# Walking the inverse's tile with heads innermost, and storing the solved inverse with blocks outermost

## The chip, the cores and the metric

One core of one Trainium2 chip runs the whole program. The metric is device microseconds (us) of one execution, from the first instruction to the last with what lies around them; a kernel's time is the median of several executions.

## The reference, cut to what matters

The first half is a recurrence over 768 steps for 4 batches x 8 heads, with a 40 x 40 state for each head; the second half is a small network on its output.

```python
for t in range(S):                       # S = 768
    y[:, :, t] = einsum('bhd,bhde->bhe', rt, state)
    Sa = einsum('bhde,bhe->bhd', state, at)
    state = state * wt[:, :, None, :] - einsum('bhd,bhe->bhde', Sa, bt)
    state = state + einsum('bhd,bhe->bhde', vt, kt)
x = y.transpose(0, 2, 1, 3).reshape(4, 768, 320)
u = x + (relu(x.T @ w_tok1) @ w_tok2).T
out = u + relu(u @ w_ch1) @ w_ch2
```

## The kernel before, in words

**The recurrence in chunks.** Time is cut into chunks of 64 steps; a group is one chunk of one batch with its 8 heads, 48 groups in all, and a pair is two neighbouring groups. Inside a chunk the steps depend on each other through a triangular 64 x 64 matrix for each head, and the kernel needs its inverse. The matrix is split into blocks of 32. The diagonal blocks of eight groups together (one set, six sets in all) are inverted by VectorE (DVE) in one go; the block off the diagonal is then put in by TensorE (PE).

**Function `t_a` (one call for each pair).** TensorE forms the products `px` (L679) in PSUM. For each half h the function `side` then issues on ScalarE (ACT): `e3`, three copies with the sign turned, from `px` into the tile `Dg` (L709), one over 128 partitions and two over 32 each; `e2` and `e4`, which copy other blocks (L691 on DVE for the first pairs, L693 on ACT later); and last, on DVE, `e1` (L699), after which the PSUM bank of `px` is given back. `Dg` is [128, 32 (s), 32 (n)]: s is the column in the block, n counts the 32 heads of the set. One `e3` writes four heads, two apart, of all 32 columns. Before the change it goes head by head: the writes step 128 bytes, the reads of `px` run in line.

**Function `t_solve` (one call for each set).** `first` (L760) is a DVE transpose of `Dg` into `DT`; a chain of small DVE steps (L782 to L818) solves into `Tl`; `o1` (L838) is a DVE transpose of `Tl` into `TBt`, the solved inverse, which reuses the tile `DT`; `o2` (L843) makes the second form `TBn`. Before the change `TBt` is [128, t, n] with the head n innermost, so the 32 values of one head's row lie 128 bytes apart. `o1` reads `Tl` in steps of 128 bytes and writes in line; `o2` does both in line.

**Users of `TBt`.** In the first two sets (16 groups) `merge` multiplies with it (`tbt`, L924) and adds a result into it (L935). For groups 0 to 23 `t_b` copies it into the block diagonal tile `TBD` in four copies of 32 x 128 (L963 on ACT, L964 on DVE) and uses it as the moving operand of the matmuls `pe` (L971). For the other 24 groups, in 12 pairs, `t_b2` does the same with copies of 32 x 256 (L1047, L1048) and matmuls `pe` (L1054). The matmuls `pt` (L999, L1084) that follow take `TBn` as the weights. `ph` (L1015, L1103) needs `TBD` whole.

**What sets the order.** A planner written in the kernel runs when the program is built: every operation carries an engine and a cost in ns written by hand, and the planner lays out one fixed order for each engine. It also puts matmuls without use (the fillers, L384) into the TensorE queue where it expects that engine to be idle. Engines run their queues in order. The costs written beside the operations are the same before and after the change.

**The rest.** `t_chain` and `t_y` carry the state from chunk to chunk; `t_mlp` is the network, whose matmuls L1567 and L1675 fill TensorE from about 340 us on, batch after batch, beside the remaining groups.

Of the kernel before, what the change touches and what calls it, by code (L numbers as in the profile page):

```python
# [13 lines left out]
AF = mybir.ActivationFunctionType  # L14
# [266 lines left out]
def tile_kernel(ctx, tc, r, k, v, w, a, b, wt1, wt2, wc1, wc2, wT, aT, kbT, vT, rT, vt, out, dbg=None):  # L281
    nc = tc.nc
# [3 lines left out]
    NP = H // 2  # L286
    NG = B * NC
    L = 32
# [29 lines left out]
    for h in range(2):  # L318
        sl = slice(h * 64, h * 64 + 64)
# [10 lines left out]
    def zbufs(shape, name, n):  # L330
        ts_ = [ctile(shape, f"{name}{i}") for i in range(n)]
        for t in ts_:
            nc.gpsimd.memset(t, 0.0)
        return ts_
# [9 lines left out]
    Tl3 = Tl[:, 0:1024].rearrange("p (j t) -> p j t", j=L)  # L344
    nc.gpsimd.memset(Tl.rearrange("p (a b) -> p a b", b=33)[:, :, 0], 1.0)
    NAB, NKP = K["nab"], K["nkp"]
    Dg = zbufs([128, L, L], "Dg", 1)[0]
# [14 lines left out]
    TBD = zbufs([128, 2 * NP, 128], "TBD", 1)[0]  # L362
# [218 lines left out]
    def noff(g):  # L581
        return NOF[g // 4][:, g % 4]
# [17 lines left out]
    def t_a(q):  # L600
        g0 = 2 * q
        si, ci = SETOF[g0]
        rank = rank_a(g0)
        early = g0 < K["eb"]
        d = {}
# [5 lines left out]
        def get_at():  # L611
            if "at" not in d:
                d["at"] = ap_.tile([128, 2 * NP, DP], F32, tag="AT", name=f"AT{q}", bufs=ATN)
                for z in range(2):
                    st[g0 + z]["at"] = d["at"][:, z * NP:(z + 1) * NP]
            return d["at"]
# [45 lines left out]
        now = yield None  # L662
# [10 lines left out]
        now = yield None  # L673
        P.rel(R_px, now)

        def pxm(z, p, h):
            def f():
                rows, cols = slice(h * 64, h * 64 + D), slice(p % 2 * 64, p % 2 * 64 + 64)
                nc.tensor.matmul(px[h][cols, 2 * z + p // 2, :], lhsT=Ac[q][rows, z, p, :], rhs=KBp[q][rows, p, z, :], start=True, stop=True)  # L679
            return ("PE", (57, 128, "E"), f)  # L680
        now = yield [pxm(z, p, h) for z in range(2) for p in range(NP) for h in (p % 2, 1 - p % 2)]
# [13 lines left out]
        def side(h):  # L695
            px_ = px[h]

            def e1():
                tt(out=get_at()[:, h::2, 0:64], in0=px_[:, :, 0:64], in1=low.unsqueeze(1).to_broadcast([128, NP, 64]), op=ALU.mult)  # L699

            def e2():
                if "n21" not in d:
                    d["n21"] = pair_n21[q] = ap_.tile([128, 2 * NP, L], F32, tag="N21", name=f"N21_{q}", bufs=ATN)
                    for z in range(2):
                        st[g0 + z]["n21"] = d["n21"][:, z * NP:(z + 1) * NP]
                neg(d["n21"][:, h::2], px_[:, :, 64:96])

            def e3(sl, c0):
                return ("ACT", 190 if sl.start == 0 else 392, lambda: nc.scalar.activation(  # L709
                    out=Dg[sl, :, ci * NP + h:(ci + 2) * NP:2].rearrange("p s n -> p n s"),  # L710
                    in_=px_[sl, :, c0:c0 + L], func=AF.Copy, scale=-1.0))

            def e4():
                o_ = NOF[g0 // 4][:, g0 % 4:g0 % 4 + 2].rearrange("p c n t -> p (c n) t")
                neg(o_[:, h::2], px_[:, :, 96:128])
            e3s = [e3(slice(0, 128), 64), e3(slice(L, 2 * L), 96), e3(slice(3 * L, 4 * L), 96)]
            if ea:
                yield [("DVE", 205, e2)] + [("DVE", 205, e4)] * (si < PEM)
                now = yield e3s
            else:  # L720
                now = yield e3s[:1] + [("ACT", 320, e2)] + e3s[1:] + [("ACT", 174, e4)] * (si < PEM)
            P.set(done[h], now)
            now = yield [("DVE", 400, e1)]
            P.rel(tks[h], now)
            yield at_ev
            now = yield None
            P.join(("at", q), 2, now, *[lambda now, z=z: P.set(AT_done[g0 + z], now) for z in range(2)])
        now = yield None
# [4 lines left out]
        now = yield None  # L733
# [10 lines left out]
    def t_solve():  # L744
        now = yield -5.0
        P.set(Dg_free[0], now)
        for i, n in enumerate(SETS):
# [7 lines left out]
            d = {}  # L755
# [5 lines left out]
            now = yield [("DVE", 1810, first)]  # L761
            P.set(Dg_free[i + 1], now)
            DT = d["DT"]
            DT3 = DT[:, 0:1024].rearrange("p (t s) -> p t s", t=L)
# [69 lines left out]
                        yield [op]  # L834

            def o1():
                TBt = DT3
                nc.vector.transpose(out=TBt, in_=Tl3.rearrange("p j t -> p t j"))  # L838
                TB[i] = [TBt]

            def o2():
# [3 lines left out]
            now = yield [("DVE", 1945, o1), ("DVE", 1158, o2)]  # L845
# [66 lines left out]
    def merge(g, ci, n21, TBt, TBn, rank):  # L912

        d = {}
        cs = slice(ci * NP, (ci + 1) * NP)
        yield rank - K["mrg"]
        yield R_et1
        d["pm"], tk = yield from bank("w", [128, 3, NP, L], f"pm{g}")

        def mm(z, lhs, rhs):  # L920
            def f1(p, q):
                def f():
                    sl = slice(q * L, (q + 1) * L)
                    nc.tensor.matmul(d["pm"][sl, z, p, :], lhsT=lhs(sl, p, q), rhs=rhs(sl, p, q), start=True, stop=True)  # L924
                return ("PE", (36, 32, "D"), f)
            return [f1(p, q) for p in range(NP) for q in range(4)]
        tbt = lambda sl, p, q: TBt[sl, :, ci * NP + p]
        tbn = lambda sl, p, q: TBn[sl, :, ci * NP + p]
        et = lambda sl, p, q: ET1[sl, p, :]
        yield mm(0, lambda sl, p, q: noff(g)[sl, p, :] if q % 2 else n21[sl, p, :], tbt)  # L930
        yield [("ACT", 260, lambda: nc.scalar.activation(out=ET1[:, :, 16:32], in_=d["pm"][:, 0, :, 16:32], func=AF.Copy, scale=half[:, 0:1]))]
        yield mm(1, tbn, et) + mm(2, et, tbn)

        def add(dst, z, c0):
            return ("DVE", 180, lambda: tt(out=dst, in0=d["pm"][:, z, :, c0:c0 + 16], in1=dst, op=ALU.add))  # L935
        now = yield [add(TBt[:, 16:32, cs].rearrange("p t n -> p n t"), 1, 16),
                     add(TBn[:, 0:16, cs].rearrange("p j n -> p n j"), 2, 0)]
        P.rel(tk, now)
        P.rel(R_et1, now)
        P.set(merged[g], now)  # L940
        yield rank

    def t_b(g):
        bi, c = divmod(g, NC)
        o = st[g]
        i, ci = SETOF[g]
# [5 lines left out]
        TBt, TBn = TB[i]  # L952
        d = {"tbd": TBD[:, g % 2 * NP:(g % 2 + 1) * NP]}
# [5 lines left out]

        def tbd(q):  # L960
            sl = slice(q * L, (q + 1) * L)
            dst, src = d["tbd"][sl, :, sl], TBt[sl, :, ci * NP:(ci + 1) * NP].rearrange("p t n -> p n t")
            ops = {"A": ("ACT", 425, lambda: nc.scalar.copy(out=dst, in_=src)),  # L963
                   "D": ("DVE", Port(285), lambda: nc.vector.tensor_copy(out=dst, in_=src)),  # L964
                   "P": ("POOL", 460, lambda: nc.gpsimd.tensor_copy(out=dst, in_=src))}
            return [ops[z] for z in K["tbd"][g >= K["tbd_early"]][q]]

        def pe(p, h):
            def f():
                q0, q1 = h * 64, h * 64 + 32  # L970
                nc.tensor.matmul(d["pe"][q0:q0 + L, p, :], lhsT=n21[q1:q1 + L, p, :],  # L971
                                 rhs=TBt[q1:q1 + L, :, ci * NP + p], start=True, stop=True)
            return ("PE", (50, 80, "D"), f)

        def etc(h):
# [12 lines left out]
        now = yield None  # L988
# [4 lines left out]
        now = yield [etc(0), etc(1)]  # L993
# [13 lines left out]
        now = yield [pt(p, h) for p in range(NP) for h in range(2)]  # L1007
        P.rel(R_et, now)
        yield tbd_done
        now = yield [tin(0), tin(1)]  # L1010
# [15 lines left out]
        now = yield [("ACT", 490, huc)]  # L1026
# [5 lines left out]
    def t_b2(q):  # L1032
        g0 = 2 * q
        i, ci = SETOF[g0]
# [5 lines left out]
        TBt, TBn = TB[i]  # L1040
        cs = slice(ci * NP, (ci + 2) * NP)
        d = {}

        def tbd(r):
            sl = slice(r * L, (r + 1) * L)
            dst, src = TBD[sl, :, sl], TBt[sl, :, cs].rearrange("p t n -> p n t")
            ops = {"A": ("ACT", 700, lambda: nc.scalar.copy(out=dst, in_=src)),  # L1047
                   "D": ("DVE", Port(490), lambda: nc.vector.tensor_copy(out=dst, in_=src))}  # L1048
            return [ops[z] for z in K["tbd"][g0 >= K["tbd_early"]][r]]

        def pe(n, h):
            def f():
                q0, q1 = h * 64, h * 64 + 32
                nc.tensor.matmul(d["pe"][q0:q0 + L, n, :], lhsT=n21[q1:q1 + L, n, :],  # L1054
                                 rhs=TBt[q1:q1 + L, :, ci * NP + n], start=True, stop=True)
            return ("PE", (50, 80, "D"), f)

        def etc(z, h):
# [14 lines left out]
        now = yield None  # L1073
# [4 lines left out]
        now = yield [etc(z, h) for z in range(2) for h in range(2)]  # L1078
# [13 lines left out]
        now = yield [pt(n, h) for n in range(2 * NP) for h in range(2)]  # L1092
        P.rel(R_et, now)
        yield tbd_done
        now = yield [tin(0), tin(1)]
        P.rel(tk, now)
        for z in range(2):
# [17 lines left out]
            now = yield [("ACT", 490, huc)]  # L1115
# [617 lines left out]
    with tc.manual_schedule():  # L1733
# [5 lines left out]
        for g in range(NG):  # L1739
            si, ci = SETOF[g]  # L1740
# [167 lines left out]
```

## Time and profile before

| what | value |
|---|---|
| median of 3 executions | 824.08 us (818.68 to 826.0) |
| profiled execution | 826.04 us, of which the span is 824.2 us |
| busy: PE, DVE, ACT | 776.5, 610.9, 486.0 us |
| mean granted TensorE clock | 0.973 |

Busy time of an engine is the time in which one of its instructions runs. Matmul ends are modelled, so a busy PE isn't PE at its peak. "Granted clock" is 1.00 at TensorE's upper level and 0.50 at its lower one. A filler counts as busy. In the lists a tile stands by its name: `DT` is the tile that `TBt` lies in, `m` and `px` are PSUM tiles.

### The profile page before, as it was taken

The page shows a single profiled execution, that of the slowest core. Times are in us where ns is not written, and L with a number is a line of the kernel's source. Part 1 is how long each engine was busy: PE and PEld are TensorE (multiplying, and loading weights), DVE is VectorE, ACT ScalarE, POOL GpSimd, SP SyncE. Part 2 cuts the span into 40 slices and gives each one's busy share as a digit, 9 for nine tenths or more (in the row PEclk, how much of TensorE's full clock was granted, in tenths as well). Part 3 has the DMA queues.
Part 4 walks back from the last instruction along what each step waited for, and adds up shares of the span by engine and source line. Part 5 has one row for each costly group of instructions (what it writes and reads, how often), then busy time and mean ns, then how long its engine had stood idle before and what let it go on. Part 6 is the DMA issues. An engine that isn't in the chain of part 4 may idle for free. (4 is left out here: it accounts for less than half of the span.)

```text
span 824.2 us, 27584 instructions
## 1 busy us (share of the span) xinstructions
PE 776.5 (94%) x11353; PEld 709.3 (86%) x11353; DVE 610.9 (74%) x1493; ACT 486.0 (59%) x1479; POOL 67.1 (8%) x143
## 2 busy tenths in 40 slices
PE   6797999888989989989999999999999999999997
PEld 6696888777878878879899899999999999998996
DVE  7999598998999878977879898499754433535342
ACT  5747887888778865765855746643654343443111
POOL 4000000000001110100101010001000010000000
PEclk9997897999999999989999999999999999999999
DMA  8964656778477975463677557244565534244341
GB/s 239 276 204 137 216 182 191 209 233 251 142 249 208 266 231 155 124 184 115 193 226 230 174 176 222 66 131 135 192 174 166 168 100 123 95 141 163 109 151 52
DMA packets 69077, 144.23 MB, mean 175 GB/s; under 512 B 8016, under 2 KB 45904, under 8 KB 65872
## 3 DMA queue, kind: packets, MB, share of 16 engines
q1 hardware_dynamic: 62608, 95.20, 39.1%
q0 software_dynamic: 6336, 47.19, 17.9%
q8 instruction: 92, 1.51, 0.8%
q14 instruction: 41, 0.34, 0.2%
HBM read 115.81 MB, written 26.54 MB: 173 GB/s over the span
## 5 line engine op out<-in xcount | busy, mean ns | idle before, releaser
L1675 PE MATMUL m<-ut,wg_c 128*128 128x384 f32 x768 | 162.5, 348 | 2.1 <-issue 2.0
L1567 PE MATMUL m<-wg_c,hd 128*128 128x320 f32 x864 | 157.3, 322 | 0.1
L1567 PEld LDWEIGHTS m<-wg_c,hd 128*128 128x128 f32 x864 | 131.3, 191 | 4.9 <-DVE hd L1687 2.2
L1675 PEld LDWEIGHTS m<-ut,wg_c 128*128 128x128 f32 x768 | 131.2, 189 | 2.2 <-DVE x L1715 0.5
L1685 ACT ACTIVATE hd<-m 128x384 fp32r<-128x384 f32 x96 | 47.2, 492 | 124.7 <-PE m L1675 118.1
L1687 DVE SCALAR_TENSOR_TENSOR hd<-m,hd 128x384 fp32r<-128x384 f32 x96 | 53.4, 556 | 57.9 <-ACT hd L1685 57.2
L1715 DVE TENSOR_TENSOR x<-m,x 128x320 f32<-128x320 f32 x96 | 46.8, 488 | 53.2 <-PE m L1567 52.5
L709 ACT ACTIVATE Dg<-px 128x128 f32<-128x128 f32 x144 | 56.5, 393 | 14.9 <-PE px L679 10.5
L1165 PE MATMUL pq<-RBs,VSs 104*104 104x128 f32 x384 | 57.8, 289 | 0.8 <-ACT VSs L1280 0.7
L1165 PEld LDWEIGHTS pq<-RBs,VSs 104*104 104x104 f32 x384 | 49.9, 180 | 3.2 <-ACT VSs L1280 1.5
L384 PE MATMUL yb<-ident 128*128 128x192 bf16 x479 | 46.3, 253 | 3.2 <-POOL ident masks.py:199 1.8
L1305 PE MATMUL yb<-KB,RM 128*64 128x40 f32 x768 | 47.3, 230 | 0.7 <-DVE RM L1222 0.7
L1307 PE MATMUL yb<-VSs,RBs 104*64 104x40 f32 x768 | 46.6, 229 | 0.0
L384 PEld LDWEIGHTS <-ident 128*128 128x128 bf16 x479 | 41.2, 101 | 4.9 <-issue 2.2
L1305 PEld LDWEIGHTS yb<-KB,RM 128*64 128x64 f32 x768 | 39.7, 137 | 4.9 <-issue 2.6
L1172 ACT COPY Gb<-pq 104x256 f32<-104x256 f32 x96 | 34.4, 373 | 15.1 <-PE pq L1165 13.6
L1307 PEld LDWEIGHTS yb<-VSs,RBs 104*64 104x64 f32 x768 | 39.7, 137 | 0.0
L397 DVE TENSOR_TENSOR cv_c<-cv_c 128x384 f32<-128x384 f32 (+3 forms) x72 | 36.5, 522 | 1.9 <-ACT cv_c L1408 1.5
L307 PE MATMUL pU<-ident,Gb 104*104 104x104 f32 x176 | 30.2, 268 | 8.0 <-DVE Gb L1259 3.5
L1200 POOL TENSOR_TENSOR RM<-Gb,upp 64x128 f32<-64x128 f32 x45 | 23.6, 531 | 169.2 <-ACT Gb L1172 169.0
L1250 PE MATMUL pS<-W2s,KB 128*40 128x40 f32 x704 | 33.6, 207 | 1.5 <-ACT W2s L1230 0.7
L307 PEld LDWEIGHTS pU<-ident,Gb 104*104 104x104 f32 x176 | 17.7, 132 | 19.1 <-ACT Gb L1263 6.5
(170 smaller groups left out, 1719.2 us busy)
## 6 DMA issues: line engine op xcount, KB each, us to landing
wg_c<-sG POOLq DMA_DIRECT2D x16, 1152.0 KB, 6.2
wg_c<-sG POOLq DMA_DIRECT2D x16, 960.0 KB, 5.4
KBp<-in_kbT_dram SPq DMA_DIRECT2D x24, 448.0 KB, 5.8
RBs<-in_rT_dram SPq DMA_DIRECT2D x48, 224.0 KB, 4.4
wg_t<-sT POOLq DMA_DIRECT2D x8, 1152.0 KB, 5.9
VSs<-in_vT_dram SPq DMA_DIRECT2D x48, 182.0 KB, 3.6
sKB<-KT SPq DMA_DIRECT2D x48, 160.0 KB, 3.1
KB<-sKB SPq DMA_DIRECT2D x48, 160.0 KB, 4.4
```

The lines of the kernel that those rows point to most:

```text
L307: nc.tensor.matmul(out_, lhsT=in_, rhs=idn, start=True, stop=True, is_transpose=True)
L384: nc.tensor.matmul(yb[:, 320:512], lhsT=zf[:, 0:128], rhs=zf[:, 0:192], start=True, stop=True)
L397: return [(e, Port(60 + f * n / 0.96 if e == "DVE" else 140 + 2.24 * n), lambda e=e: engines[e].tensor_tensor(out=out_(), in0=a_(), in1=b_ ...
L709: return ("ACT", 190 if sl.start == 0 else 392, lambda: nc.scalar.activation(out=Dg[sl, :, ci * NP + h:(ci + 2) * NP:2].rearrange("p s n - ...
L1165: nc.tensor.matmul(stepped(d["pq"][0:DP, p, 0:64], 144, 2), lhsT=vs[:, gi * 2 + p, :], rhs=rb[:, gi * 2 + p, :].rearrange("p (h t) -> p h ...
L1305: nc.tensor.matmul(dst, lhsT=rms[g - 1 + z][:, h, :], rhs=o["kb"][:, h, :], start=True, stop=False)
L1307: nc.tensor.matmul(dst, lhsT=o["rb"][:, h // 2, q0:q0 + 64], rhs=o["vs"][:, h // 2, 64:DP], start=False, stop=True)
L1567: nc.tensor.matmul(d[key], lhsT=lhs(i, a_), rhs=rhs(i, b_), start=i == 0 and j == 0, stop=i == n - 1 and j == 2)
L1675: nc.tensor.matmul(pt, lhsT=mm_[q][0], rhs=mm_[q][1], start=q == 0, stop=q == len(mm_) - 1)
L1685: nc.scalar.activation(out=hid[key][:, 0], in_=pt, func=AF.Relu)
L1687: now = yield [("DVE", dve(TB_), lambda: nc.vector.scalar_tensor_tensor(out=hid[key][:, 1], in0=pt, scalar=0.0, in1=hid[key][:, 0].bitcast ...
L1715: now = yield [("DVE", dve(320), lambda: tt(out=x()[:, i], in0=d[("c2", g, i)], in1=x()[:, i], op=ALU.add))]
```

## The change

Two layouts are turned, and nothing is added or taken away: the number and the order of the instructions stay.

- `e3`: the same elements go from `px` to `Dg`, in another order. Now the four heads are innermost: writes in runs of four, 8 bytes apart, then a step of 128 bytes; reads of `px` in PSUM step 512 bytes inside a run.
- `o1`: `TBt` is now [128, n, t], blocks outermost. The transpose still reads `Tl` in steps of 128 bytes and now also writes in steps of 128 bytes.
- Every user of `TBt` takes the new view, so that it reads (and in L935 also writes) in line: `tbt` of the matmuls L924, the first addition of L935, the copies L963, L964, L1047 and L1048, the moving operand of L971 and L1054.

```diff
             def e3(sl, c0):
                 return ("ACT", 190 if sl.start == 0 else 392, lambda: nc.scalar.activation(
-                    out=Dg[sl, :, ci * NP + h:(ci + 2) * NP:2].rearrange("p s n -> p n s"),
-                    in_=px_[sl, :, c0:c0 + L], func=AF.Copy, scale=-1.0))
+                    out=Dg[sl, :, ci * NP + h:(ci + 2) * NP:2],
+                    in_=px_[sl, :, c0:c0 + L].rearrange("p n s -> p s n"), func=AF.Copy, scale=-1.0))
...
             def o1():
-                TBt = DT3
-                nc.vector.transpose(out=TBt, in_=Tl3.rearrange("p j t -> p t j"))
+                TBt = DT[:, 0:1024].rearrange("p (n t) -> p n t", t=L)
+                nc.vector.transpose(out=TBt.rearrange("p n t -> p t n"), in_=Tl3.rearrange("p j t -> p t j"))
...
-        tbt = lambda sl, p, q: TBt[sl, :, ci * NP + p]
+        tbt = lambda sl, p, q: TBt[sl, ci * NP + p, :]
...
-        now = yield [add(TBt[:, 16:32, cs].rearrange("p t n -> p n t"), 1, 16),
+        now = yield [add(TBt[:, cs, 16:32], 1, 16),
...
-            dst, src = d["tbd"][sl, :, sl], TBt[sl, :, ci * NP:(ci + 1) * NP].rearrange("p t n -> p n t")
+            dst, src = d["tbd"][sl, :, sl], TBt[sl, ci * NP:(ci + 1) * NP]
...
-                                 rhs=TBt[q1:q1 + L, :, ci * NP + p], start=True, stop=True)
+                                 rhs=TBt[q1:q1 + L, ci * NP + p, :], start=True, stop=True)
...
-            dst, src = TBD[sl, :, sl], TBt[sl, :, cs].rearrange("p t n -> p n t")
+            dst, src = TBD[sl, :, sl], TBt[sl, cs]
...
-                                 rhs=TBt[q1:q1 + L, :, ci * NP + n], start=True, stop=True)
+                                 rhs=TBt[q1:q1 + L, ci * NP + n, :], start=True, stop=True)
```

## Rows read from the trace of the kernel before

**Rows 1.** Page: busy time with share and count; granted clock in 40 slices.

```profile
PE 776.5 (94%) x11353; PEld 709.3 (86%) x11353; DVE 610.9 (74%) x1493; ACT 486.0 (59%) x1479; POOL 67.1 (8%) x143
...
PEclk9997897999999999989999999999999999999999
```

**Rows 2.** Windows: length; busy PE, PEld, DVE, ACT, POOL; granted clock; DMA share; GB/s.

```profile
0.00:60.00 60.00, 47.74 (x626) 43.61 (x627) 55.18 (x130) 36.56 (x103) 10.64 (x32) 1.00 0.85 242
60.00:340.00 280.00, 256.94 (x5140) 226.07 (x5137) 245.06 (x614) 216.69 (x691) 16.27 (x31) 0.94 0.69 206
340.00:600.00 260.00, 255.02 (x3407) 235.69 (x3406) 212.64 (x503) 154.00 (x463) 24.65 (x50) 0.98 0.53 164
600.00:745.00 145.00, 143.60 (x1728) 132.40 (x1726) 65.88 (x181) 63.76 (x187) 11.84 (x23) 1.00 0.46 136
```

**Rows 3.** Groups by line and form: total us, mean ns; idle before. `e3`.

```profile
L709 ACT ACTIVATE Dg<-px 32x128 f32<-32x128 f32 x96 | 37.4, 390 | 1.5
...
L709 ACT ACTIVATE Dg<-px 128x128 f32<-128x128 f32 x48 | 19.1, 398 | 13.4 <-PE px L679 10.5 <-DVE noff L691 2.3
```

**Rows 4.** Timeline, 33 to 37 us: start, length, instruction, idle before it.

```profile
33.23 2.46 ACT L709 ACTIVATE Dg<-px 128x128 f32<-128x128 f32 x6
...
35.96 0.42 DVE L699 TENSOR_TENSOR AT<-px,low 128x256 f32<-128x256 f32 x1
...
36.14 0.90 PE L307 MATMUL pk<-ident,KBp 104*128 104x104 f32 x8 [1.37 <-ACT Dg L709]
36.29 1.97 DVE L760 STREAM_TRANSPOSE DT<-Dg 128x1024 f32<-128x1024 f32 x1
```

**Rows 5.** Groups by line and form: copies, additions, transposes of the inverse.

```profile
L963 ACT COPY TBD<-DT 32x128 f32<-32x128 f32 x53 | 21.8, 412 | 3.1 <-DVE DT L935 2.3
...
L1047 ACT COPY TBD<-DT 32x256 f32<-32x256 f32 x28 | 18.2, 649 | 0.4
...
L838 DVE STREAM_TRANSPOSE DT<-Tl 128x1024 f32<-128x1024 f32 x6 | 12.0, 1998 | 0.0
...
L964 DVE COPY TBD<-DT 32x128 f32<-32x128 f32 x43 | 11.7, 272 | 0.7
...
L1048 DVE COPY TBD<-DT 32x256 f32<-32x256 f32 x20 | 7.6, 378 | 0.4
L843 DVE STREAM_TRANSPOSE TBn<-Tl 128x1024 f32<-128x1024 f32 x6 | 7.4, 1226 | 0.0
...
L935 DVE TENSOR_TENSOR DT<-pm,DT 128x64 f32<-128x64 f32 x16 | 4.4, 274 | 3.4 <-PE pm L924 3.3
```

**Rows 6.** Groups by line and form: the nearest instructions without long steps.

```profile
L1005 ACT COPY TBD<-pt 32x128 f32<-32x128 f32 x48 | 12.2, 255 | 1.1 <-PE pt L999 0.5
...
L1260 DVE TENSOR_TENSOR Gb<-pS,PC 40x80 f32<-40x80 f32 x44 | 10.3, 234 | 0.7
...
L1402 ACT ACTIVATE cv_c<-cv_c 128x384 f32<-128x384 f32 x12 | 6.7, 558 | 0.5 <-DMA cv_c<-in_moe_w_ch_dram 0.4
...
L1402 ACT ACTIVATE cv_c<-cv_c 128x320 f32<-128x320 f32 x12 | 6.0, 500 | 0.1
...
L1403 DVE TENSOR_SCALAR cv_c<-cv_c 128x384 int32<-128x384 int32 x12 | 4.2, 353 | 0.1
...
L1403 DVE TENSOR_SCALAR cv_c<-cv_c 128x320 int32<-128x320 int32 x12 | 3.8, 318 | 0.0
...
L693 ACT ACTIVATE noff<-px 128x128 f32<-128x128 f32 x8 | 2.2, 278 | 0.1
```

**Rows 7.** Groups by line and form: the small matmuls of the later pairs.

```profile
L1084 PE MATMUL pt<-ET,TBn 32*32 32x32 f32 x384 | 13.1, 217 | 0.0
L1054 PE MATMUL pe<-DT,N 32*32 32x32 f32 x384 | 13.1, 228 | 0.0
```

**Rows 8.** Chain that ended last, in order of time: start, length, what.

```profile
711.53 1.00 PE pe L1054 x32
```

**Rows 9.** Windows, columns as in rows 2: one stretch with a low clock.

```profile
120.00:140.00 20.00, 18.82 (x362) 16.62 (x360) 16.41 (x47) 13.52 (x44) 0.00 (x0) 0.74 0.64 187
```

## The prediction, made before the changed kernel was run

> **What bounds the kernel now.** I read the page's busy time first, then a table of windows by stage, then the groups by line and form, and a piece of the timeline where an engine waits for a touched line. TensorE is busy 94% of the span [rows 1], so the question is when it is not. The windows answer it [rows 2]. In 340 to 600 and 600 to 745 us it is idle 260.00 - 255.02 = 5.0 and 145.00 - 143.60 = 1.4 us: there only work taken from TensorE itself shortens anything, and DVE and ACT have room. In the first 60 us it is idle 12.3 us, in 60 to 340 us 23.1 us, and here DVE is busy 92% and 88%, ACT 61% and 77%. So time given back on DVE and ACT before 340 us can reach the end, up to these 35 us of idle time, and after 340 us nearly none of it. The touched lines and their durations are in [rows 3], [rows 5] and [rows 7]; [rows 4] shows that one of them, L709, stands on a path in the prologue: six `e3` in a row take 2.46 us, the last `e1` (L699) comes behind them, and both TensorE's next transposes (idle 1.37 us) and the first set's transpose L760 start after it. The granted clock is a second bound: it falls to the lower level in a few stretches before 420 us [rows 1, 9], and in them a busy TensorE does its work at half speed.
>
> **The change part by part.** The number and order of the instructions stay, and no wait is added or removed, no queue is passed. What changes is how long each takes. I sum against the profiled execution, 826.04 us, and take the same sum off the median of 824.08, which is 0.24% less.
>
> *`e3`, 144 instructions.* Now 390 ns over 32 partitions and 398 over 128 [rows 3], with writes in steps of 128 bytes. The same engine evicting the same size from PSUM with writes in line takes 255 (L1005) and 278 ns (L693) [rows 6], so the write step costs some 120 to 135 ns. After the change the writes come in runs of four, 8 bytes apart. A run through SBUF in 8-byte steps is shown by L1402, as a read: 558 ns for 384 and 500 for 320 elements, 0.91 ns for each more, no dearer than it should be, so I expect the write penalty to go. But the reads of PSUM now step 512 bytes, which no row shows. Bounds: 255 (a read for free) and 390 + 135 = 525 ns (the read pays what the write paid, and the write keeps paying). I take 280 ns, near the rows from PSUM without long steps, since the step that these rows show as dear is one of SBUF; -0.11 us each.
> Prologue (36 of the 144): six in a row lose 0.66 us; the last six before L760 pass that on [rows 4], earlier pairs only in part, since DVE is 92% busy beside them. Value -1.0 us, bounds 0 and -2.6 (four pairs of 0.66). In 60 to 340 us 66 of them give ACT 7.3 us; the 42 later ones lie beside a busy TensorE and count nothing.
>
> *Copies into `TBD`.* On ACT 412 ns for 128 and 649 for 256 elements [rows 5]: 1.85 ns for each more element, against 0.91 in L1402. Carried down, L1402 gives 326 and 442 ns; L1005's 255 is the lower end. I take 326 and 442: -86 ns x 53 = -4.6 us, of which 50 copies (-4.3) lie before 340 us, and -207 ns x 28 = -5.8 us, all after 340 us. On DVE 272 and 378 ns; L1403, one source and one output in SBUF, costs 0.55 ns for each more element and gives 213 and 283: -59 x 43 = -2.5 us and -95 x 20 = -1.9 us (the latter after 340 us). No gain at all would be the other end.
>
> *`o1` and the addition L935.* `o1` reads in 128-byte steps and takes 1998 ns where `o2`, in line, takes 1226 [rows 5]: 0.75 ns for each element. With the write stepped too it could stay (+0) or add as much again (+0.77 us). L935 of before is the nearest row: it reads and writes `TBt` in 128-byte steps and takes 274 ns for 64 elements, against 234 for 80 in L1260, or about 217 for 64. That is 0.89 ns for each element for both steps together; they overlap. So `o1` goes to about 1226 + 0.89 x 1024 = 2.14 us, +0.14 us x 6, three of them before 340 us: +0.4. L935 loses its 57 ns: 16 x 0.057 = -0.9 us.
>
> *What of this reaches the end in 60 to 340 us.* ACT gets 7.3 + 4.3 = 11.6 us back of 216.7, DVE 2.5 + 0.9 - 0.4 = 3.0 of 245.1. Counted only where TensorE happens to be idle (8% of the stretch) that is 1.2 us; were every microsecond on the path, more than 11. Waits gather where these engines are late, so I take one and a half times the former: -1.8 us, bounds 0 and -8. The rest hides under TensorE's own work and its fillers, whose number is fixed; what is late next is TensorE itself.
>
> *Small matmuls.* The moving operand of `pe` now lies in line. The rows show 228 ns for L1054 and 217 for L1084, whose moving operand is in line already [rows 7]: 11 ns, with two instructions side by side, so 32 x 11 / 2 = 0.18 us in a block of 32, which takes 1.00 us of the chain [rows 8]. Twelve such blocks lie in the stretch that TensorE bounds: -2.1 us. Matmul ends are modelled and L1084 carries a stepped weight tile, so the bounds are 0 and -6 us (half of each block). The 24 half blocks of L971 and the 16 first rounds of L924 give at most 24 x 0.09 + 16 x 0.09 = 3.6 us where TensorE is also waiting; I take -0.5.
>
> Sum: -1.0 - 1.8 - 2.1 - 0.5 = -5.4 us, or 820.6 for the profiled execution and 818.7 from the median; I say 819.
>
> **A rule against it.** Before, `e3` read PSUM in line and paid at the write [rows 3]. The Trainium skill, PSUM — Partial Sum Buffer, Specifications (TRN2), says that PSUM has lines of 8 bytes and that any pattern that isn't contiguous slows matmuls significantly; it says so of matmuls, and no run here shows ACT reading PSUM in steps. By it the stepped read would eat the gain of `e3`, and the sum would be that of the first rival below.
>
> **The rivals.**
> *`e3` keeps its time*, because the stepped read costs what the stepped write cost. For it: a 128-byte step is dear wherever these rows have one, at about 1 ns for each element. Against: all those are steps in SBUF. Then -1.0 falls out and of the -1.8 some two thirds: -1.0 - 1.2 = 2.2 us less, a gain of 3.2, 821.
> *`e3` grows, slower than before.* The place is ACT's queue before 340 us. At 525 ns, +135 each, the prologue's six in a row take 0.8 us more in four pairs (+3.2) and 66 x 0.135 = 8.9 us are added to ACT in 60 to 340 us, of which I count half, since `e1`, the PSUM bank and the copies into `TBD` queue behind: +4.5. Against it stand 3.2 us from the other parts: +4.5, 828.6. It decides from about +57 ns on, an `e3` of some 450 ns.
> *Nothing reaches the end.* The savings fall into slack: TensorE's queue holds 479 fillers at fixed places, and ACT and DVE wait for TensorE as well. Moving operands cost the same in line. 824.
> *The clock.* The stretch 120 to 140 us had a granted clock of 0.74 [rows 9], so 26% x 20 x 2 = 10.4 us at the lower level, in which a TensorE that is busy nearly all the time loses about 5 us; it follows idle time of TensorE that the change shortens. If this stretch and one of the others of its kind go, 8 us come on top of part of the sum: 811. New low stretches are as possible; then the sum is given back, which is the case before this one.
>
> **How the numbers follow.** Forecast 0.35, `e3` unchanged 0.25, nothing reaches 0.15, the clock 0.15, `e3` grows 0.10. A measurement of this kernel tells about 1% (8 us) from no change: faster means under 815.8, slower over 832.3. Faster: 0.35 x 0.25 + 0.15 x 0.9 + 0.25 x 0.1 = 0.25. Slower: 0.10 x 0.4 + (0.15 + 0.25) x 0.06 = 0.06, say 0.07. The rest, 0.68, lies within 1%. The range takes in the clock's case on one side and the grown `e3` on the other: 809 to 828.
>
> **What would show it right or wrong.** Right: L709 near 280 ns in both forms; L963 and L1047 near 326 and 442, L964 and L1048 near 213 and 283; L838 between 2.0 and 2.2 us; the chain's blocks of `pe` near 0.8 us; TensorE's idle time in 60 to 340 us below 23 us by some 2 us, and after 340 us as before. The first rival shows as L709 near 390 ns, the slower one as L709 over 450 with ACT's busy time in 60 to 340 us above 217 us. Wrong would be all durations as forecast and the end unmoved, or an end moved by more than 8 us with a granted clock far from 0.973: then it wasn't the instructions but the clock's stretches that decided.

## The result and the profile after

The changed kernel takes 812.88 us (median of 19 executions, 805.55 to 819.46), the kernel before in the same series 824.18 (19 executions, 816.45 to 829.65). The ratio is 0.9874, 95% interval 0.9844 to 0.9904: 1.3% faster, about 10 us. (The ratio leaves out executions over 1.5% slower than their kernel's fastest, so it isn't the quotient of the two medians.) The forecast was 819, so the direction held and the size was about half. The profiled execution took 811.58 us, with a span of 809.8 us and a mean granted clock of 0.974, beside 826.04, 824.2 and 0.973 before: the mean clock, then, isn't what changed.

Page of the changed kernel: busy time with share and count, and the granted clock in 40 slices.

```profile
PE 763.6 (94%) x11353; PEld 699.1 (86%) x11353; DVE 605.8 (75%) x1493; ACT 459.4 (57%) x1479; POOL 66.7 (8%) x143
...
PEclk9997799889999999999999999999999999999999
```

Against [rows 1], ACT lost 26.6 us of busy time and DVE 5.1; TensorE lost 12.9, nearly all of the 14.4 us by which the span shrank, while its idle time went only from 47.7 to 46.2 us. In this pair of executions the work of the engine that bounded the kernel has become shorter, hardly its waits.

Groups by line and form of the changed kernel: total us, mean ns, idle before.

```profile
L709 ACT ACTIVATE Dg<-px 32x128 f32<-32x128 f32 x96 | 26.5, 276 | 1.5
L963 ACT COPY TBD<-DT 32x128 f32<-32x128 f32 x53 | 15.6, 294 | 3.2 <-DVE DT L935 2.3
L709 ACT ACTIVATE Dg<-px 128x128 f32<-128x128 f32 x48 | 13.6, 283 | 14.8 <-PE px L679 11.3 <-DVE noff L691 2.9
L1084 PE MATMUL pt<-ET,TBn 32*32 32x32 f32 x384 | 13.1, 217 | 0.0
L838 DVE STREAM_TRANSPOSE DT<-Tl 128x1024 f32<-128x1024 f32 x6 | 12.9, 2148 | 0.0
...
L971 PE MATMUL pe<-DT,N 32*32 32x32 f32 x384 | 11.8, 196 | 1.6 <-DVE DT L935 1.4 <-issue 0.3
L1047 ACT COPY TBD<-DT 32x256 f32<-32x256 f32 x28 | 11.2, 402 | 0.4
...
L964 DVE COPY TBD<-DT 32x128 f32<-32x128 f32 x43 | 9.2, 215 | 0.7
...
L924 PE MATMUL pm<-DT,noff 32*32 32x32 f32 x256 | 8.7, 204 | 0.0
...
L1054 PE MATMUL pe<-DT,N 32*32 32x32 f32 x384 | 8.5, 192 | 0.0
...
L924 PE MATMUL pm<-DT,N 32*32 32x32 f32 x256 | 8.3, 201 | 2.0 <-DVE AT L699 2.0
...
L1048 DVE COPY TBD<-DT 32x256 f32<-32x256 f32 x20 | 5.6, 280 | 0.9 <-PE ph L1103 0.5
...
L935 DVE TENSOR_TENSOR DT<-pm,DT 128x64 f32<-128x64 f32 x16 | 3.5, 221 | 2.9 <-ACT Gb L898 2.4 <-PE pm L924 0.3
```

These answer to [rows 3], [rows 5] and [rows 7]. `e3` went from 390 and 398 to 276 and 283 ns, the copies on ACT from 412 to 294 and from 649 to 402, those on DVE from 272 to 215 and from 378 to 280, the addition from 274 to 221, and `o1` rose from 1998 to 2148. L1054 went from 228 to 192, while L1084, which the change doesn't touch, stayed at 217.

The early matmuls that read `TBt`, in the kernel before:

```profile
L971 PE MATMUL pe<-DT,N 32*32 32x32 f32 x384 | 16.0, 227 | 1.6 <-DVE DT L935 1.1 <-ACT HU L1020 0.3 <-issue 0.2
...
L924 PE MATMUL pm<-DT,N 32*32 32x32 f32 x256 | 10.7, 227 | 1.9 <-DVE AT L699 1.9
L924 PE MATMUL pm<-DT,noff 32*32 32x32 f32 x256 | 10.6, 227 | 0.0
```

L1054 lost 4.6 us of TensorE's time, L971 4.2 and the first round of L924 4.3. Together that is 13.1 us: in this pair the matmuls whose moving operand was turned account for what TensorE lost.

Chain that ended last, changed kernel, near its end: start, length, what.

```profile
697.46 0.62 PE pe L1054 x32
...
704.32 1.03 PE pt L1084 x32
```

This is the line that matters. A block of 32 `pe` takes 0.62 us of the chain where [rows 8] has 1.00: 0.38 us saved, twice the 0.18 of the forecast. (The kernel issues 16 matmuls for a pair; the trace has two records for each, and "32" counts records.)

Timeline of the changed kernel around the six `e3` of [rows 4]: start, length, instruction, idle before it.

```profile
33.00 1.78 ACT L709 ACTIVATE Dg<-px 128x128 f32<-128x128 f32 x6
...
34.51 1.21 DVE L397 TENSOR_TENSOR KBp<-KBp,w 104x1024 f32<-104x1024 f32 x1
35.65 0.41 DVE L699 TENSOR_TENSOR AT<-px,low 128x256 f32<-128x256 f32 x1
...
35.83 0.91 PE L307 MATMUL pk<-ident,KBp 104*128 104x104 f32 x8 [1.29 <-issue]
35.98 1.99 DVE L760 STREAM_TRANSPOSE DT<-Dg 128x1024 f32<-128x1024 f32 x1
```

Against [rows 4] the six `e3` take 1.78 us, not 2.46, but L699 and L760 start only 0.31 us sooner, and 0.23 of that was there when the first of the six started. So of the 0.68 us saved hardly any is passed on. DVE is busy with L397 up to L699 (34.51 + 1.21 = 35.72), and that was so in the kernel before:

```profile
34.83 1.22 DVE L397 TENSOR_TENSOR KBp<-KBp,w 104x1024 f32<-104x1024 f32 x1
```

There the last `e3` ended at 33.23 + 2.46 = 35.69 us and L397 at 36.05, and L397 writes `KBp`, which TensorE's next transposes read; they start 0.09 us after it there and 0.11 us after it here. What L699 and those transposes came behind was DVE's L397, not `e3`, though the row names L709.

**Where the time went.** The fixed stages of [rows 2] don't compare well, for everything moves forward and a fixed window holds other work in the two kernels. So the windows below are cut at the same work, at the starts of the fifth and sixth L838. First the kernel before, then the changed one: window and its length; busy PE, PEld, DVE, ACT, POOL; granted clock; DMA share; GB/s.

```profile
495.90:583.80 87.90, 87.79 (x1101) 81.98 (x1100) 71.26 (x168) 45.08 (x126) 7.70 (x16) 1.00 0.47 145
583.80:824.20 240.40, 232.79 (x2407) 218.89 (x2405) 108.24 (x268) 89.86 (x258) 17.13 (x33) 1.00 0.43 134
```

```profile
484.60:571.00 86.40, 86.19 (x1099) 80.39 (x1099) 70.82 (x169) 41.53 (x126) 7.68 (x16) 1.00 0.46 147
571.00:809.80 238.80, 231.29 (x2408) 217.85 (x2406) 107.75 (x268) 87.05 (x258) 17.08 (x33) 1.00 0.44 135
```

The clock is at its upper level in all four. Each stretch has four of the twelve late `pe` blocks, and each is 1.5 to 1.6 us shorter: 1.60 and 1.50 us of TensorE's busy time, with its idle time as it was (0.1 and 0.2, 7.6 and 7.5 us). That is 0.4 us a block, the 0.38 of the chain, and it counts whole.

### The profile page after: what moved, and what is told of

Its sections match the earlier page's. It is cut to its first block, busy times and chain, and to the rows that moved or that the text cites. A ratio compares the mean times of both kernels' runs of the same rounds, so it can differ in the third digit from the quotient of the medians.

```text
span 809.8 us, 27584 instructions
## 1 busy us (share of the span) xinstructions
PE 763.6 (94%) x11353; PEld 699.1 (86%) x11353; DVE 605.8 (75%) x1493; ACT 459.4 (57%) x1479; POOL 66.7 (8%) x143
## 4 chain that ended last, share of the span: by engine, by line
PE 68%; DVE 13%; ACT 9%; issue 4%; DMA 4%; POOL 1%; SPq 0%; ACTq 0%; POOLq 0%; DVEq 0%
PE m L1567 19%; PE m L1675 16%; PE pq L1165 4%; PE pq L1191 3%; PE ph L1103 2%; PE yb L1305 2%; PE yb L1307 2%; PE pU L307 2%; PE px L679 2%; PE pk L307 2%; PE pq L1186 2%; PE ph L1015 2%; PE pm L924 1%; PE pS L1250 1%; DVE cp L487 1%
## 5 line engine op out<-in xcount | busy, mean ns | idle before, releaser
L1567 PE MATMUL m<-wg_c,hd 128*128 128x320 f32 x864 | 155.0, 319 | 0.0
L1567 PEld LDWEIGHTS m<-wg_c,hd 128*128 128x128 f32 x864 | 129.2, 188 | 4.0 <-DVE hd L1687 1.8
L1165 PEld LDWEIGHTS pq<-RBs,VSs 104*104 104x104 f32 x384 | 49.2, 177 | 2.5 <-ACT VSs L1280 1.1
L709 ACT ACTIVATE Dg<-px 128x128 f32<-128x128 f32 x144 | 40.1, 278 | 16.3 <-PE px L679 11.3
L397 DVE TENSOR_TENSOR cv_c<-cv_c 128x384 f32<-128x384 f32 (+3 forms) x72 | 36.5, 522 | 1.9 <-ACT cv_c L1408 1.7
L1280 ACT COPY VSs<-pU 104x80 f32<-104x80 f32 x88 | 18.4, 226 | 28.3 <-PE pU L307 27.4
```

The lines of the kernel that those rows point to most:

```text
L1165: nc.tensor.matmul(stepped(d["pq"][0:DP, p, 0:64], 144, 2), lhsT=vs[:, gi * 2 + p, :], rhs=rb[:, gi * 2 + p, :].rearrange("p (h t) -> p h ...
L1567: nc.tensor.matmul(d[key], lhsT=lhs(i, a_), rhs=rhs(i, b_), start=i == 0 and j == 0, stop=i == n - 1 and j == 2)
```

## The experiments

Three theories stood after the result. M: the small matmuls were mis-sized. R: the relief of ACT and DVE before 340 us was. C: the clock's low stretches differ by chance or by the change.

**A common measure.** The time of one and the same kernel moves with the granted clock that an execution got, and medians of 6 to 12 executions carry that: the layout without `e3`, run twice, gave ratios of 0.9878 and 0.9979 at mean clocks of 0.976 and 0.969. So beside each ratio stands the time at equal clock. It is a straight line of time against granted clock through all 209 executions whose clock is known, one slope for all kernels and one height for each. The slope is -6.5 us for each 0.01 of clock (-6.6 on the kernel before alone, 75 executions), the scatter about the lines 2.1 us. (Through the 177 executions that the ratios use the slope is -5.7, and no entry of the last column moves by more than 1.2 us.) The runs came from three chips, on which the kernel before takes 823.5, 822.9 and 823.4 us at equal clock. At a clock of 0.973 the kernel before takes 823.3 us; the others stand against that, with intervals of two standard errors:

| kernel | median us | ratio to before, 95% | us against before, at equal clock |
|---|---|---|---|
| the change | 812.88 | 0.984 to 0.990 | -9.4 ± 1.1 |
| e3 alone | 824.07 | 0.995 to 1.003 | -1.1 ± 1.3 |
| layout alone, first run | 815.96 | 0.982 to 0.994 | -6.1 ± 1.8 |
| layout alone, second run | 819.65 | 0.994 to 1.002 | -5.6 ± 1.3 |
| change, all its matmuls stepped | 821.46 | 0.994 to 1.002 | -2.9 ± 1.3 |
| before, only late `pe` in line | 819.97 | 0.983 to 0.995 | -4.1 ± 1.8 |
| change, late `pe` stepped | 820.34 | 0.995 to 1.002 | -4.7 ± 1.3 |
| change, early matmuls stepped | 817.17 | 0.989 to 0.996 | -6.3 ± 1.3 |
| change, all copies stepped | 821.06 | 0.993 to 0.999 | -5.6 ± 1.3 |
| change, early copies stepped | 818.94 | 0.991 to 0.999 | -6.1 ± 1.3 |
| change, late copies stepped | 813.77 | 0.982 to 0.992 | -9.0 ± 1.8 |
| before, 128-partition `e3` twice | 836.54 | 1.008 to 1.017 | +12.1 ± 1.8 |
| change, `TBn` blocks outermost too | 811.88 | 0.977 to 0.985 | -9.7 ± 1.7 |

"Early" is groups 0 to 23, "late" 24 to 47. "Stepped" operands are read from `TBn`, which has the head innermost as `TBt` had before.

**`e3` alone.** Before, with the first hunk of the change:

```diff
-                    out=Dg[sl, :, ci * NP + h:(ci + 2) * NP:2].rearrange("p s n -> p n s"),
-                    in_=px_[sl, :, c0:c0 + L], func=AF.Copy, scale=-1.0))
+                    out=Dg[sl, :, ci * NP + h:(ci + 2) * NP:2],
+                    in_=px_[sl, :, c0:c0 + L].rearrange("p n s -> p s n"), func=AF.Copy, scale=-1.0))
```

> The kernel before with the new walk of e3 alone. L709 near 278 ns as in the changed kernel. Theory M (the matmuls were the mis-sized term: a block of pe in line takes 0.62 us and not 0.82): e3 gives what the prediction gave it, about 2.2 us, so 822 against 824. Theory R (the relief of ACT and DVE before 340 us was the mis-sized term): e3 alone gives 4 to 6 us, 818 to 820. Theory C (the clock): TensorE's idle time before 340 us as before, time different only as far as the granted clock is.

L709 took 275 and 281 ns, as in the changed kernel; 16.6 us of ACT's work went (37.4 + 19.1 in [rows 3], 39.9 left), and 1.1 ± 1.3 us at the end, where theory R had 4 to 6.

**The layout alone.** The changed kernel with that hunk undone.

> The changed kernel with e3 as before: the layout of the solved inverse alone. Theory M: nearly all of the gain is kept, 8 to 9.5 us of 11.3, so about 815. Theory R: 5 to 7 us, about 818.

> The changed kernel with e3 in its old walk (the layout of the inverse alone), a second time, to size what e3 gives beside the rest. Compared at equal granted clock. If e3 counts as the prediction has it (1.0 in the prologue and 0.9 of the relief): +1.9 us over the changed kernel. If e3 gives nothing, as in the run with e3 alone: 0 to +1 us. If it gives more once the rest is faster: +3 us or more. L709 390 and 398 ns.

The two runs together give -5.8 ± 1.1, which is what theory R gave the layout, and not M. So in the changed kernel `e3` is worth 3.6 ± 1.5 us, against 1.1 ± 1.3 alone; the forecast's 1.9 to 2.2 lies between.

**Matmuls stepped again, all of them.** The same tile supplies `tbt`; L971 and L1054 read it likewise.

```diff
-        tbt = lambda sl, p, q: TBt[sl, ci * NP + p, :]
+        tbt = lambda sl, p, q: TBn[sl, :, ci * NP + p]
...
-                                 rhs=TBt[q1:q1 + L, ci * NP + n, :], start=True, stop=True)
+                                 rhs=TBn[q1:q1 + L, :, ci * NP + n], start=True, stop=True)
```

> The changed kernel, but the moving operand of pe and of the first round of merge is read out of the other form of the inverse, TBn, in steps of 128 bytes as before the change (the values are other ones, so the output isn't that of the reference; order and waits of the instructions are the same). Blocks of pe back at 1.00 us. Theory M: 6 to 8 us of the gain are lost, so 819 to 821. Theory R: 3 to 5 us are lost (4.6 in the twelve late blocks at most), 816 to 818.

The block is back at 1.00 us and 6.5 ± 1.7 us of the 9.4 are gone: most of the gain hangs on the matmuls' operand.

**Only the late `pe` in line (in the kernel before), and the late `pe` alone stepped (in the changed one).** One line each; the second reads `TBn` there, as in the last hunk above, and the first is:

```diff
-                                 rhs=TBt[q1:q1 + L, :, ci * NP + n], start=True, stop=True)
+                                 rhs=TBt[q1:q1 + L, ci * NP + n, :], start=True, stop=True)
```

> The kernel before, with only the moving operand of the twelve late blocks of pe (L1054) read in line: it reads a row of the old layout, so the values are other ones and the output isn't that of the reference. Both theories: blocks at 0.62 us and 12 x 0.38 = 4.6 us less, 819.6, since TensorE is busy all the time there. If the time stays, TensorE wasn't the bound after 340 us.

> The changed kernel, but the moving operand of the 12 late pe blocks (L1054) is read from the second form of the inverse in steps of 128 bytes; the early matmuls stay in line. The values of pe differ. Compared at equal granted clock. If each block's 0.38 us counts whole: the block 1.00 us again and +4.6 us over the changed kernel (theory M). If the prediction's size was right: +2.1 us. If the late blocks count nothing and the gain of the matmuls is all early: 0 to +1 us.

Put in alone it gives 4.1 ± 1.8, taken out alone 4.7 ± 1.7 (the difference of two lines of the table), and 12 blocks at 0.38 us make 4.6. Windows of the kernel with the late `pe` stepped, from its fifth L838 and from its sixth:

```profile
488.80:576.70 87.90, 87.65 (x1100) 81.86 (x1099) 70.73 (x169) 41.55 (x126) 7.66 (x16) 1.00 0.47 144
576.70:817.40 240.70, 232.75 (x2408) 219.08 (x2406) 107.80 (x268) 87.05 (x258) 17.09 (x33) 0.99 0.44 134
```

TensorE's busy time and both lengths are those of the kernel before again, though ACT's 41.55 and 87.05 us are as in the changed kernel: in these stretches ACT's relief is worth nothing and the operand everything.

**Early matmuls stepped** (`tbt` and L971; L1054 in line).

> The changed kernel, but the moving operand of the half blocks of pe before 360 us (L971) and of merge's first round (L924) is read out of TBn in steps of 128 bytes; the late blocks (L1054) stay in line (other values, so the output isn't that of the reference). Theory M: the late blocks are worth 12 x 0.38 = 4.6 us, and what they leave of the 11.3, some 4 to 6 us, is lost here: 817 to 819. Against it: before 360 us TensorE also waits, so that its shorter blocks fall into waits; then 813 to 814.

3.1 ± 1.7 us go, where theory M had 4 to 6 and its rival none.

**The copies stepped again:** all, the early ones, the late ones.

```diff
-            dst, src = d["tbd"][sl, :, sl], TBt[sl, ci * NP:(ci + 1) * NP]
+            dst, src = d["tbd"][sl, :, sl], TBn[sl, :, ci * NP:(ci + 1) * NP].rearrange("p t n -> p n t")
...
-            dst, src = TBD[sl, :, sl], TBt[sl, cs]
+            dst, src = TBD[sl, :, sl], TBn[sl, :, cs].rearrange("p t n -> p n t")
```

> The changed kernel, but the copies into TBD (L963, L964, L1047, L1048) read TBn in steps of 128 bytes, so they take 412, 272, 649 and 378 ns again (other values, so the output isn't that of the reference). Theory M (only the matmuls' time reaches the end): no change against the changed kernel, 813 +- 2. Theory R (relief of ACT and DVE reaches the end in part): 1 to 2 us lost, 814 to 815. By the prediction's own value (two thirds of one and a half times the idle share) 0.7 us.

> The changed kernel, but the copies of groups 0 to 23 (L963, L964) read the second form of the inverse in steps of 128 bytes, as all copies did before; the later copies stay in line. TBD gets other values. Compared at equal granted clock (a line through all executions, time against clock). Theory P (before 340 us ACT and DVE set TensorE's waits, so that a copy's time there counts about half): L963 411 and L964 272 ns again, 53 x 0.12 + 43 x 0.06 = 8.9 us of work, and +3 to +4.5 us over the changed kernel, which is the whole loss seen with all copies stepped. Theory Q (the copies' loss came from the later groups, whose TBD is waited for by ph): 0 to +1 us. Theory S (half from each): about +2 us.

> The changed kernel, but the copies of groups 24 to 47 (L1047, L1048) read the second form of the inverse in steps of 128 bytes; the early copies stay in line. TBD gets other values. Compared at equal granted clock. The prediction counted these copies at nothing, since TensorE is busy beside them: then 0 to +1 us (theory P), with L1047 649 and L1048 381 ns and TensorE's idle time after 340 us unchanged. Theory Q: +3 to +4 us, and TensorE waits for TBD before L1103. Theory S: about +2 us.

All: 3.8 ± 1.7 us go, where theory M had none. Early: 3.3 ± 1.7. Late: 0.5 ± 2.1. That is theory P. Groups by form with the early copies stepped, and then with the late ones:

```profile
L963 ACT COPY TBD<-TBn 32x128 f32<-32x128 f32 x53 | 21.9, 413 | 3.5 <-DVE TBn L935 2.7
...
L964 DVE COPY TBD<-TBn 32x128 f32<-32x128 f32 x43 | 11.6, 270 | 0.7
```

```profile
L1047 ACT COPY TBD<-TBn 32x256 f32<-32x256 f32 x28 | 18.2, 650 | 0.6 <-DVE TBn L843 0.2
...
L1048 DVE COPY TBD<-TBn 32x256 f32<-32x256 f32 x20 | 7.6, 382 | 0.9 <-PE ph L1103 0.5
```

Stepping costs as much work in both places, 21.9 - 15.6 + 11.6 - 9.2 = 8.7 us and 18.2 - 11.2 + 7.6 - 5.6 = 9.0. Before 340 us it costs about 3 us of time, beside a busy TensorE none that can be measured.

**`e3` over 128 partitions issued twice** in the kernel before: 48 x 398 ns = 19.1 us more on ACT.

```diff
-                return ("ACT", 190 if sl.start == 0 else 392, lambda: nc.scalar.activation(
+                return ("ACT", 190 if sl.start == 0 else 392, lambda: [nc.scalar.activation(
...
-                    in_=px_[sl, :, c0:c0 + L], func=AF.Copy, scale=-1.0))
+                    in_=px_[sl, :, c0:c0 + L], func=AF.Copy, scale=-1.0) for _ in range(1 + (sl.start == 0))])
```

> The kernel before, with the 128-partition e3 issued twice (the same copy again, 48 more instructions of about 390 ns, 18.7 us more work on ACT, of which 34 and 13.3 us before 340 us; the output stays that of the reference). If ACT has slack before 340 us, as theory M says: under 3 us more, up to 827. If ACT stands on the path there (so that e3's lost gain must have another cause): 5 to 10 us more, 829 to 834.

+12.1 ± 1.8 us, two thirds of what was added and more than either expectation. In the profiled executions 8.8 of the 11.1 us are lost by the fourth L838, which starts at 379.5 us after 370.7, and in the kernel before 34 of the 48 `e3` over 128 partitions (13.5 us) lie before 340 us. So ACT's work there is nearly on the path when it grows, and the slack that theory M counted on is refuted. The first L838 alone gives no price: it starts at 67.9 us where it stood at 62.0, 5.9 us for 4.8 us of work (12 `e3`), but in this execution the clock fell on the way. The kernel before and this one, 30 to 41 us, columns as in [rows 2]:

```profile
30.00:41.00 11.00, 8.84 (x136) 7.81 (x136) 10.80 (x23) 7.18 (x22) 1.04 (x1) 1.00 0.89 248
```

```profile
30.00:41.00 11.00, 8.73 (x81) 7.64 (x80) 7.78 (x15) 6.75 (x20) 1.04 (x1) 0.69 0.68 205
```

**`TBn` with blocks outermost as well**, from the changed kernel, so that the weights of `pt` are in line too; L924, L935 and L999 are turned in the same way, and their lines are left out here:

```diff
-                nc.vector.transpose(out=TBn.rearrange("p s n -> p (s n)"), in_=Tl[:, 0:1024])
+                nc.vector.transpose(out=TBn.rearrange("p n s -> p s n"), in_=Tl3)
...
-                nc.tensor.matmul(d["pt"][q0:q0 + L, n, :], lhsT=TBn[q0:q0 + L, :, ci * NP + n],
+                nc.tensor.matmul(d["pt"][q0:q0 + L, n, :], lhsT=TBn[q0:q0 + L, ci * NP + n, :],
```

> The changed kernel with TBn, the other form of the inverse, laid out blocks outermost too: o2 writes in steps of 128 bytes (about 2.0 us for 1.23, six times), and the weights of pt and of merge's second round and the moving operand of its third lie in line. The output stays that of the reference. Theory M: blocks of pt go from 1.03 to about 0.65 us, 12 x 0.38 = 4.6 us less in the late part and 2 to 4 us less before, less 1 to 2 for o2: 805 to 808. If a stepped weight load hides behind the matmuls beside it: blocks of pt stay, 813 to 815.

Groups by form, and the window from its sixth L838:

```profile
L843 DVE STREAM_TRANSPOSE TBn<-Tl 128x1024 f32<-128x1024 f32 x6 | 12.0, 1998 | 0.0
...
L1084 PE MATMUL pt<-ET,TBn 32*32 32x32 f32 x384 | 8.3, 192 | 0.0
```

```profile
583.20:822.40 239.20, 229.62 (x2405) 215.84 (x2403) 108.46 (x268) 86.91 (x258) 17.08 (x33) 0.99 0.44 135
```

It has the best median, but at equal clock it isn't told from the change (-9.7 ± 1.7 and -9.4 ± 1.1), and theory M's 805 to 808 didn't come. The blocks of `pt` shrank as `pe` had (in the chain from 1.03 to 0.62 us, L1084 from 217 to 192 ns), and TensorE's busy time in this window fell by 1.67 us, from 231.29; yet the window got no shorter, 239.20 after 238.80, for the idle time rose from 7.5 to 9.6 (its clock was below the upper level only in the last 18 us, 0.92 after 0.98, where TensorE is partly idle in both). The waits of TensorE in the window say for whom:

```profile
PE pU L307 <- ACT Gb L898: 1.2, 1, 1.2
...
PE pU L307 <- DVE Gb L1260: 0.9, 1, 0.9
```

In the changed kernel the same window has 0.3 us of waiting for L898 and none for L1260. So there the chain that carries `Gb` from chunk to chunk may have taken the gain back. That is a pointer and not shown: the profiled execution, 824.15 us at a mean clock of 0.961, is far above this kernel's median, and the 0.77 us by which each L843 has grown on DVE can have eaten gain before this window; no run parts the two.

**The theories.** C falls: at equal clock 9.4 us of the gain remain, and the two kernels' mean clocks, 0.973 over 19 and 0.972 over 75 executions, differ by about 1 us in the line. M holds, and gives half of the gain from the late blocks alone. R holds in part: the early copies and `e3` cost 3.3 and 3.6 us when taken out of the changed kernel, as much as the early matmuls' 3.1.

## Why the prediction was half right

**Right.** Durations: L709 276 and 283 ns (280 forecast), L964 215 (213), L1048 280 (283), `o1` 2.148 us (2.14), L935 53 ns less (57). ACT's copies came out a tenth shorter than forecast, L963 294 (326) and L1047 402 (442). The rivals in which `e3` keeps its time or grows fell, and so did the one in which nothing reaches the end. The stepped read of PSUM takes 276 ns over 32 partitions and 283 over 128, against 255 and 278 for the reads in line of [rows 6]. The Trainium skill, PSUM — Partial Sum Buffer, Specifications (TRN2), states its slowing for matmuls only, and the trace doesn't extend it to ACT. That the copies after 340 us count nothing held too, within 2 us.

**Wrong: the path of `e3` in the prologue.** The prologue's term was -1.0, because the last six `e3` were read out of [rows 4] as what L699, L760 and TensorE's transposes wait for. They wait for DVE's L397, as shown above, and of the 0.66 us for six hardly any is passed on there. Still the first L838 starts at 61.5 us, 0.5 us sooner; where that was won isn't shown. With its share of the relief, 0.9 (half, as 7.3 of 14.6 us; the first rival takes two thirds, 1.2), the forecast for `e3` was 1.9 to 2.2, between the 1.1 and 3.6 that were measured: the sum for `e3` came near by luck.

**Wrong: the small matmuls, the main step.** "11 ns, with two instructions side by side, so 32 x 11 / 2 = 0.18 us in a block" measured 0.38, by the chain, by two windows and by two runs. The 11 ns came from L1084 as the row "in line", but L1084's weight tile is itself stepped; the text named this and used it only for the bound. The run with `TBn` turned shows what L1084 is in line: 192 ns, not 217. The row taken for the clean one carried the same penalty, 1.03 us a block where 0.62 is clean. The halving failed too: by it the 36 ns between 228 and 192 would be 0.58 us of a block. So the twelve blocks give 4.1 to 4.7 us, not 2.1.

**Wrong: the early parts.** The early matmuls stood at 0.5 us, with 3.6 as the most they could give, and cost 3.1 ± 1.7 when taken out. That bound was too low: it took a first round of L924 for half a block, but 512 records in 16 groups are 32 each, a whole one, and TensorE's time in L971 and this round fell by 4.2 + 4.3 = 8.5 us. Not all of that reached the end; in which stage it was lost isn't shown. The early copies had at most half of ACT's and DVE's relief of 1.8, and cost 3.3 ± 1.7. The factor "one and a half times" the share of idle time was too low, and adding the terms was the wrong form. One at a time, `e3`, the early matmuls and the early copies cost 3.6 + 3.1 + 3.3 = 10.0 ± 3.5 us when taken out; together they can only be the 9.4 less the 4.1 to 4.7 of the late blocks, some 5 us; and `e3` alone gave 1.1. This is what a path would show that runs through ACT, DVE and TensorE in turn, where any of them left slow holds back the others, but that is argued: neither the early matmuls alone nor the early copies alone was put into the kernel before. TensorE's idle time, in single executions, points to it without settling it: 46.2 us in the changed kernel, 54.2 and 49.2 with `e3` in its old walk, 50.7 with the early copies stepped, but 47.4 with all of them. It stays open how the 5 us divide.

**The sign by which it was to be read.** "TensorE's idle time in 60 to 340 us below 23 us by some 2 us" failed: it is 24.6 (280 - 255.44), in a kernel that is faster.

```profile
60.00:340.00 280.00, 255.44 (x5151) 226.46 (x5149) 244.62 (x618) 207.47 (x697) 16.47 (x31) 0.93 0.69 206
```

The fixed window now holds other work. Cut at the same work, from the first L838 to the fourth, before and after:

```profile
62.01:370.72 308.71, 283.01 (x5507) 249.22 (x5505) 268.01 (x670) 236.76 (x758) 18.68 (x35) 0.94 0.67 199
```

```profile
61.52:364.33 302.81, 278.25 (x5513) 246.76 (x5511) 265.94 (x670) 223.99 (x757) 18.38 (x35) 0.93 0.67 201
```

TensorE's idle time fell from 25.7 to 24.6 us, half of the 2 us of the sign, and its busy time by 4.8.

**The clock.** In the changed kernel 120 to 140 us has a granted clock of 0.91 where [rows 9] has 0.74, but low stretches lie elsewhere instead. From the first L838 to the second and on to the third, before and after:

```profile
62.01:146.75 84.74, 76.76 (x1737) 66.76 (x1736) 70.48 (x190) 66.10 (x207) 1.24 (x2) 0.84 0.60 181
146.75:243.94 97.19, 87.13 (x2092) 76.65 (x2088) 89.75 (x234) 78.66 (x248) 2.29 (x6) 0.96 0.72 214
```

```profile
61.52:143.13 81.61, 72.76 (x1733) 63.96 (x1730) 69.59 (x189) 63.05 (x207) 1.24 (x2) 0.85 0.63 187
143.13:241.72 98.59, 88.04 (x2096) 77.56 (x2094) 89.00 (x233) 74.98 (x247) 2.33 (x6) 0.93 0.71 210
```

Over the whole execution the mean stayed, 0.973 and 0.974. That rival fell.

## What to carry to other kernels

Where one engine is busy nearly all the time, cost its own instructions first and best: a change of layout made for copies paid most through the operand of small matmuls that stood beside them. Before a row is taken as the price of the clean form, look at each of its operands; if the other one has the same fault, the difference of the two rows is no price, and the chain's length of a whole block is the better measure. Before a row's named releaser is taken for the path, look when it ended: L709 had ended 0.45 us before the transposes that were put down to it. And cut windows at the same work, not at the same time, and compare executions at equal clock before a difference of one per cent is read.

## What was not expected

- One stepped operand costs a block of 32 small matmuls 0.38 us (1.00 against 0.62), the stepped weights of `pt` about as much (1.03 against 0.62): L1084's busy time fell from 13.1 to 8.3 us when they were turned, L1054's from 13.1 to 8.5 with the moving operand.
- ACT pays for steps of 128 bytes in SBUF, 412 against 294 ns for 128 elements and 649 against 402 for 256, and hardly anything for steps of 512 bytes in PSUM: `e3` takes 276 and 283 ns, reads in line 255 and 278.
- An instruction that the change doesn't touch got shorter: the copies of L693 into `N`, which stand between `e3` copies on ACT, take 318 and 273 ns before and after, 272 with `e3` alone turned and 317 and 319 with the layout alone. So a stepped write of `e3` lengthens the record of its neighbour as well.
- The DVE transpose takes 1.23 us with both sides in line, 2.00 with one stepped, be it the read (L838 before) or the write (L843 with `TBn` turned), and 2.15 with both (L838 after). The second step costs 0.15 us where the first costs 0.77. The Trainium skill, Vector Engine (DVE) Microarchitecture Reference, Measured stream behaviour on trn2, says of an elementwise instruction with two sources that read and write penalties only partly add; these rows show it for the transpose.
- Work added to ACT and work taken from it aren't mirror images: 19.1 us more cost 12.1 ± 1.8, 16.6 us less gave 1.1 ± 1.3.
